# Merging a kernel's DMA transposes in pairs, with a new order of its work

## The chip, the cores and the metric

The kernel runs on one core of a Trainium2 chip. The metric is the device time of one execution in microseconds; three runs of the kernel before took 324.96, 324.96 and 325.57 us, the median is 324.96 us.

## The reference

One block of a transformer whose normalisations and residuals are modulated by a conditioning vector c. S = 2048 rows, D = 640, 32 heads of 20, F = 1536, all in bf16:

```python
mod = (silu(c) @ w_mod)            # six rows of 640: sa, ca, ga, sb, cb, gb
h = layernorm(x) * (1 + ca) + sa
q, k, v = split(h @ wqkv)          # 32 heads of 20
scores = q k^T / sqrt(20), masked to 0 <= i - j < 256
x = x + ga * (softmax(scores) v @ wo)
h = layernorm(x) * (1 + cb) + sb
x = x + gb * ((sigmoid(h @ w_gate) * (h @ w_up)) @ w_down)
```

## The kernel before, in words

**Tiling.** The 2048 rows are cut into 8 chunks of 256 rows, each of two blocks of 128. All weights lie in SBUF once they are loaded. Each chunk goes through these steps, and the steps of several chunks overlap:

- *ln1*: VectorE (DVE) takes each row's statistics (L773, L775), GpSimd (POOL) the power (L778, L780), and x is normalised (L793, or L790 on POOL).
- *hT*: the normalised rows are turned to 640 x 256. For chunks 0 to 2 (NPH = 3) TensorE (PE) does it; from chunk 3 on a DMA transpose for each block (transp_dma, L800, issued by SP). Then scale and shift are applied (modulate, L808 on ACT, L809 on DVE or POOL; L848/L849 where PE turned).
- *qkv*: chains of 5 matmuls (pe_chain, L686) project a block; ACT or DVE casts the result out of PSUM (evac, L884/L885): V into its tile, Q and K into stg, padded to 32 columns a head. stg is turned, for chunks 0 and 1 (NPQ = 2) by PE (matmuls on ident), else by one DMA transpose for Q into QT and one for K into KT.
- *attention*: sets of score matmuls into the one PSUM tile S (four banks); ACT takes the exponentials (E, L995), POOL masks the edges of the window (L1020), a burst of matmuls (pvs, M<-E,V) sums the values, DVE turns and divides (L1064, L1069, L1071, L1073). The rows are written to a DRAM buffer (doc) and read back turned (oT).
- *wo*, residual (L1125), *ln2*, and x2 turned into h2T by DMA transposes, two for each chunk.
- *mlp*: per pair of column tiles the chains g and u (M<-h2T,wg and M<-h2T,wu), tanh on ACT (L1170), the product hh on DVE ("glu", L1172), and at the chunk's end the down chains (M<-wd,hh), which need all of hh; then the residual (L1191) and the store.

**The modulation rows.** The first two (scale and shift of ln1) are needed at once: c is turned (L651), silu is formed (L653 to L655), spread over MW = 64 columns (silubc, L657), and fifty matmuls give mA ("modA"). The other four come in two groups in mod_rows: a group of 20 matmuls (modb, M<-wu,silubc and M<-hh,silubc), a transpose that gives shB or scB, and for the gate a scaled copy gq (L730), a DMA to a DRAM row (gate<-gq), and a DMA that reads this row onto all partitions (gbc<-gate). The first gate is multiplied into wo's five tiles (L1214), the second into wd's twelve (L1153), on DVE or POOL.

**What sets the order.** All operations and their engines stand in one table PRIO: the number of an operation gives its rank, its last digit (modulo 5) its engine. schedule() goes through them in that order, hands out the slots of the tile pools (M has four PSUM banks), and emit() writes each engine's program, with waits on semaphores. Each engine works off its program in order; an instruction that waits holds up all behind it. Nearly all DMAs are issued by SP, a few by ACT; a tile's slot passes on only when its last reader is done.

Of the kernel before, what the change touches and what calls it, by code (L numbers as in the profile page):

```python
# [8 lines left out]
ALU = mybir.AluOpType  # L9
# [352 lines left out]
def c_pe(n):  # L362
# [117 lines left out]
]  # L480
TR1 = 2
NPH = 3
NPQ = 2
PQ = ()
KEEP = 3
DSAFE = 0.3
RING = 256
FETCH = 3.3
START = 0.8
PORTLAG = 0.05  # L490
# [776 lines left out]
```

## Time and profile before

| what | value |
|---|---|
| median of 3 runs | 324.96 us |
| profiled execution, its own time | 324.87 us |
| its span in the trace | 323.1 us |
| granted TensorE clock | 1.00 |
| busiest engines | PE 317.6 us, ACT 216.1, DVE 210.0, POOL 177.3 |
| DMA issues on SP that transpose | 50 |

The span is the time from the first to the last recorded instruction; the execution's own time is 1.8 us longer. Times in the trace count from the span's start. PEld is PE's load of the stationary operand, which runs beside the matmuls; an engine with a "q" is its queue, where DMAs are issued. In a row of the timeline stand start, duration, engine, line, operation, tiles written and read, shape, count, and in brackets the idle time before it with what ended it.

### The profile page before, as it was taken

Reading aid. Unit: us, or ns where it says so; the run is one execution under the profiler, and the core shown is the slowest. Engines: PE = TensorE matmul, PEld = TensorE weight load, DVE = VectorE, ACT = ScalarE, POOL = GpSimd, SP = SyncE. Lnnn points to the kernel's source line nnn. Section 1 sums busy time; section 2 is a strip of 40 time slices with the busy share of each in tenths; the row PEclk is TensorE's granted clock in tenths of the full one; section 3 lists DMA queues with packets and bytes.
Section 4 is the critical chain, followed back from the end, with each engine's and each line's share of the span. In section 5 each row is a group of like instructions: output and inputs, shape, how many; then the busy total and the mean of one; then the engine's idle time right before and its main releaser. Section 6 shows DMA issues by size and latency. Waiting matters only on the chain.

```text
span 323.1 us, 11621 instructions
## 1 busy us (share of the span) xinstructions
PE 317.6 (98%) x4879; PEld 223.5 (69%) x4879; DVE 210.0 (65%) x420; ACT 216.1 (67%) x322; POOL 177.3 (55%) x267
## 2 busy tenths in 40 slices
PE   8999999999999999999999999999999999999997
PEld 3665545556776578766776567877786788877885
DVE  3799987897789856784757365647554576473332
ACT  2697887888766879976869877867778764112220
POOL 4146869868749593948393947582749273012000
PEclk9999999999999999999999999999999999999999
DMA  7989698989962275524325363410311021303001
GB/s 250 372 291 374 131 199 178 136 201 331 228 100 69 63 104 124 104 47 116 93 47 77 97 115 90 109 46 4 87 49 50 27 42 59 109 0 84 20 22 41
DMA packets 71039, 37.85 MB, mean 117 GB/s; under 512 B 45259, under 2 KB 69067, under 8 KB 70987
## 3 DMA queue, kind: packets, MB, share of 16 engines
q1 hardware_dynamic: 69680, 35.64, 46.1%
q10 hardware_dynamic: 1306, 1.48, 1.5%
q8 instruction: 38, 0.62, 0.8%
q14 instruction: 15, 0.11, 0.1%
HBM read 21.30 MB, written 5.25 MB: 82 GB/s over the span
## 4 chain that ended last, share of the span: by engine, by line
PE 90%; DVE 3%; DMA 2%; POOL 2%; issue 2%; ACT 1%; DVEq 0%; POOLq 0%
PE M L686 73%; PE S L687 7%; PE M L687 6%; PE S L666 2%; POOL E L1020 1%; DMA gbc<-gate 1%; DMA gate<-gq 1%; PE S L686 1%; ACT E L995 0%; POOL st L780 0%; DVE hh L1172 0%; DVE x L793 0%; DVE stg L885 0%; DVE KT L885 0%; DVE wo L1214 0%
## 5 line engine op out<-in xcount | busy, mean ns | idle before, releaser
L995 ACT ACTIVATE E<-S 128x512 bf16<-128x512 f32 (+2 forms) x184 | 150.2, 877 | 40.0 <-PE S L687 35.9
L1020 POOL TENSOR_SCALAR_AFFINE_SELECT E<-E 128x512 bf16<-128x512 bf16 (+1 forms) x176 | 138.8, 818 | 67.2 <-ACT E L995 30.1
L686 PE MATMUL M<-wqkv,hT 128*128 128x480 bf16 (+1 forms) x340 | 71.5, 355 | 0.9 <-DVE hT L809 0.6
L686 PE MATMUL M<-h2T,wg 128*128 128x256 bf16 x480 | 64.1, 273 | 0.0
L686 PE MATMUL M<-h2T,wu 128*128 128x256 bf16 x480 | 63.5, 273 | 0.0
L1172 DVE SCALAR_TENSOR_TENSOR hh<-sig,M 128x512 bf16<-128x512 f32 x48 | 32.0, 677 | 40.3 <-ACT sig L1170 29.6
L686 PE MATMUL M<-wd,hh 128*128 128x320 bf16 (+2 forms) x396 | 57.2, 295 | 0.2
L1170 ACT ACTIVATE sig<-M 128x512 f32<-128x512 f32 x48 | 28.7, 599 | 39.7 <-PE M L686 31.7
L686 PEld LDWEIGHTS M<-h2T,wg 128*128 128x128 bf16 x480 | 45.8, 98 | 7.4 <-issue 0.2
L686 PEld LDWEIGHTS M<-wqkv,hT 128*128 128x128 bf16 x340 | 30.8, 98 | 28.4 <-DMA wqkv<-in_A_wqkv_dram 0.9
L686 PEld LDWEIGHTS M<-h2T,wu 128*128 128x128 bf16 x480 | 45.4, 98 | 6.8 <-issue 0.2
L686 PEld LDWEIGHTS M<-wd,hh 128*128 128x128 bf16 x396 | 37.1, 98 | 14.5 <-DVE hh L1172 0.9
L1191 DVE TENSOR_TENSOR x<-M,x 128x320 bf16<-128x320 f32 (+2 forms) x33 | 15.3, 474 | 28.6 <-PE M L686 28.3
L687 PEld LDWEIGHTS S<-QT,KT 20*64 20x64 bf16 (+1 forms) x1856 | 19.9, 100 | 19.8 <-issue 8.4
L687 PE MATMUL S<-QT,KT 20*64 20x256 bf16 (+5 forms) x1856 | 32.1, 228 | 0.0
L773 DVE BATCH_NORM_STATS2 st<-x 128x6 f32<-128x320 bf16 x64 | 28.7, 479 | 3.5 <-DMA x<-in_A_x_dram 3.1
L1064 DVE STREAM_TRANSPOSE T<-M 128x512 f32<-128x512 f32 x32 | 21.1, 694 | 7.2 <-PE M L687 7.1
L686 PE MATMUL M<-wo,oT 128*128 128x320 bf16 x160 | 24.9, 299 | 0.0
L687 PE MATMUL M<-E,V 128*32 128x128 bf16 (+1 forms) x960 | 22.8, 246 | 0.5 <-DVE shB L738 0.3
L687 PEld LDWEIGHTS M<-E,V 128*32 128x32 bf16 x960 | 19.0, 97 | 4.9 <-POOL E L1020 2.4
L778 POOL TENSOR_SCALAR st<-st 128x2 f32<-128x2 f32 x16 | 3.6, 226 | 32.6 <-DVE st L775 31.8
L1125 DVE TENSOR_TENSOR x<-M,x 128x320 bf16<-128x320 f32 x32 | 15.5, 486 | 8.3 <-PE M L686 7.7
(75 smaller groups left out, 240.8 us busy)
## 6 DMA issues: line engine op xcount, KB each, us to landing
x<-in_A_x_dram SPq DMA_DIRECT2D x21, 160.0 KB, 3.5
doc<-On SPq DMA_DIRECT2D x64, 40.0 KB
wd<-in_B_w_down_dram SPq DMA_DIRECT2D x4, 480.0 KB, 4.3
out_dram<-x SPq DMA_DIRECT2D x11, 160.0 KB, 1.8
wd<-in_w_mod_dram SPq DMA_DIRECT2D x5, 320.0 KB
wqkv<-in_A_wqkv_dram SPq DMA_DIRECT2D x4, 400.0 KB, 7.9
wu<-in_w_mod_dram SPq DMA_DIRECT2D x5, 320.0 KB
oT<-doc SPq DMA_DIRECT2D x8, 192.0 KB, 2.5
```

What stands on the lines that cost most here:

```text
L666: ins = e.matmul(p_S.aps[0][:, 3, :], Eall[:, 0, 0:128], Eall[:, 0, 128:640], start=True, stop=True)
L686: return e.matmul(o, l, r, start=st, stop=sp, skip_group_check=True)
L687: return e.matmul(o, l, r, start=st, stop=sp, tile_position=tp, skip_group_check=True)
L773: A("dve", lambda e, g, bi=bi, j=j: e.bn_stats(v(bi * 12 + j * 6, 6), src[bi].ap[:, j * 320:(j + 1) * 320]), 0.48, reads=[src[bi].r()], wr ...
L778: A("pool", lambda e, g: e.tensor_scalar(v(28, n), var(), EPS, None, op0=ALU.add), 0.2, reads=[st.r(("m", bi)) for bi in range(n)], writes ...
L995: A("act", lambda e, eng: e.activation(dst(), src(), ACT.Exp, scale=SM_SCALE), c_act(n), reads=[Sp.r()], writes=[E.r(key)], prio=3, tag=f" ...
L1020: A("pool", lambda e, eng: e.affine_select(rows(dst), rows(src), pattern=[[0, 8], [sign, n]], compare_op=ALU.is_ge, fill=0.0, base=base, c ...
L1064: A("dve", lambda e, g, h=h: e.transpose(T1.ap[:, 512 * h:512 * h + 512], X[h].ap), 0.694, reads=[X[h].r()], writes=[T1.r(h)], prio=3.5, t ...
L1125: A("dve", lambda e, g, ps=ps, bi=bi, half=half: e.tensor_tensor(x1[bi].ap[:, half * 320:half * 320 + 320], ps.ap[:, 0:320], x1[bi].ap[:, ...
L1170: A("act", lambda e, g, pg=pg, sg=sg: e.activation(sg.ap[:], pg.ap[:], ACT.Tanh, scale=0.5), c_act(512), reads=[pg.r()], writes=[sg.r()], ...
L1172: A("dve", lambda e, g, pu=pu, sg=sg, f0=f0: e.scalar_tensor_tensor(out=hh.ap[:, f0:f0 + 2, :], in0=sg.ap[:].rearrange("p (a b) -> p a b", ...
L1191: A("dve", lambda e, g, ps=ps, bi=bi, c0=c0, n=n: e.tensor_tensor(x1[bi].ap[:, c0:c0 + n], ps.ap[:, 0:n], x1[bi].ap[:, c0:c0 + n], op=ALU. ...
```

## The change

- **hT and h2T**: one DMA transpose turns both blocks of a chunk, instead of one for each. The tiles are laid out [128, block, 5, 128] instead of [128, 5, 256], so operations on 256 columns now see two pieces of 128. x0 and x2 lie in one buffer each, whose slots are handed out in pairs (pairup).
- **Q and K**: one DMA transpose turns Q and K of a block, from two neighbouring stg slots into one tile QK that holds both. The pools QT (3) and KT (4) become one pool QK (4).
- **x** from chunk 3 on is read by one DMA per chunk.
- **Small buffers** are saved: MW is 32 instead of 64, cth lives in Dr, and gq in a slot of sig. A small load ("touch") into sig's second slot is issued by ACT; that slot is free only after it.
- **PRIO** is a new table. The count of operations on PE stays at 920 and of matmuls at 4880; ACT has 333 operations (331), DVE 422 (420), POOL 249 (255), SP 173 (200).

The core of the diff:

```diff
-    138, 143, 233, 128, 653, 33, 1593, 183, 573, 398, 38, 243, 318, 112, 163, 578, 151, 49, 166, 54, 59, 64, 69, 74,
+    83, 88, 193, 1173, 318, 983, 1008, 223, 1438, 313, 918, 287, 178, 278, 113, 598, 3466, 46, 4, 151, 24, 14, 19, 34,
...
-MW = 64
+MW = 32
...
-    p_hT = sbpool("hT", 2, [128, NDT, CH])
-    p_h2 = sbpool("h2T", 2, [128, NDT, CH])
+    p_hT = sbpool("hT", 2, [128, 2, NDT, 128])
+    p_h2 = sbpool("h2T", 2, [128, 2, NDT, 128])
...
-    p_QT = sbpool("QT", 3, [128, NG, CH])
-    p_KT = sbpool("KT", 4, [128, NG, CH])
+    p_QK = sbpool("QK", 4, [128, 2 * NG, CH])
...
+    def pairup(u, v):
+        u.mate, v.mate, v.odd = v, u, 1
...
+    touch = p_sig.aps[1][:].bitcast(BF16)
+    dma(lambda: touch[0:10, 0:32], lambda: w_mod[0:640:64, 0:32], 0.02, writes=[R("touch")], prio=-1, eng="act", nonc=True, tag="touch")
+    p_sig.init[1].append(P.ops[-1])
...
-        A("dve", lambda e, g: e.tensor_scalar(gq[:], ps.ap[:, 160 * gate:160 * gate + 160], factor, None, op0=ALU.mult), c_dve(160),
-          reads=[ps.r()], writes=[R_gq], prio=8, tag="gq")
+        gt = Tile(p_sig, "gq")
+        gq = lambda: gt.ap[:].bitcast(BF16)
+        A("dve", lambda e, g: e.tensor_scalar(gq()[:, 0:160], ps.ap[:, 160 * gate:160 * gate + 160], factor, None, op0=ALU.mult), c_dve(160),
+          reads=[ps.r()], writes=[gt.r()], prio=8, tag="gq")
...
-                ap = dst.ap[:, dt, :]
+                ap = dst.ap[:, :, dt, :]
...
-            turned[a] = [transp_dma(lambda bi=bi: t.ap[:, :, bi * 128:(bi + 1) * 128], lambda bi=bi: src[bi].ap[:], 4, 0.29,
-                                    [src[bi].r()], [t.r(("t", bi))], 1.26, f"atr{a}") for bi in range(2)]
+            turned[a] = [transp_dma(lambda: t.ap[:].rearrange("p b t c -> p (b t) c"),
+                                    lambda: x0all[:, src[0].slot:src[0].slot + 2, :].rearrange("p b c -> p (b c)"), 4, TW1,
+                                    [x.r() for x in src], [t.r(("t", bi)) for bi in range(2)], 1.28, f"atr{a}")]
...
-                else:
-                    transp_dma(lambda dst=dst, bi=bi: dst.ap[:, :, bi * 128:bi * 128 + 128], lambda s=s: s.ap[:], 3, 0.87,
-                               [s.r(i) for i in range(4)], [dst.r((bi, 0)), dst.r((bi, 1))], 1.28, f"qkt{a}")
+                elif g0:
+                    transp_dma(lambda dst=dst, bi=bi: dst.ap[:, :, bi * 128:bi * 128 + 128],
+                               lambda sq=sq: bass.AP(stgall, sq.slot * 1024, [[4096, 128], [1, 2048]]), 3, TW2,
+                               [x.r(i) for x in (sq, sk) for i in range(4)], [dst.r((g, bi, h)) for g in (0, NG) for h in range(2)], 1.6, f"qkt{a}")
...
-                    ps.ap[:, i * CH:(i + 1) * CH], w[:, kt, (f0 + i) * 128:(f0 + i + 1) * 128], h2.ap[:, kt, :]))
+                    ps.ap[:, i * CH:(i + 1) * CH], w[:, kt, (f0 + i) * 128:(f0 + i + 1) * 128], h2.ap[:, :, kt, :]))
```

What the new table moves, at the places where waits were found in the trace. First DVE's program where the first gate is multiplied into wo; M is the PSUM pool, T<-M x2 the two transposes of chunk 0's second pvs, stg and V the casts of chunk 2's projections. Before:

```order
L809 TENSOR_SCALAR hT<-hT,mA 128x256
L1064 STREAM_TRANSPOSE T<-M 128x512 x2
L1069 RECIPROCAL Dr<-T 128x32
L1071 TENSOR_TENSOR Tn<-T,Dr 128x32x20
L885 CAST stg<-M 128x24x20
L885 CAST V<-M 128x8x20
L1214 TENSOR_TENSOR wo<-wo,gbc 128x640 x2
L885 CAST stg<-M 128x24x20
L730 TENSOR_SCALAR gq<-M 128x160
```

And after, at the same place of DVE's program (sig in the first row is the second gate's gq):

```order
L734 TENSOR_SCALAR sig<-M 128x160
L741 STREAM_TRANSPOSE T<-M 128x160
L742 TENSOR_SCALAR scB<-T 128x5
L1078 STREAM_TRANSPOSE T<-M 128x512 x2
L1228 TENSOR_TENSOR wo<-wo,gbc 128x640
L897 CAST stg<-M 128x16x20
L897 CAST V<-M 128x8x20
L1083 RECIPROCAL Dr<-T 128x32
L1085 TENSOR_TENSOR Tn<-T,Dr 128x32x20
L1228 TENSOR_TENSOR wo<-wo,gbc 128x640 x2
```

The first scaling of wo now stands ahead of the casts stg and V, and of the reciprocal; the second gate's gq, which stood behind the first two scalings, stands ahead of the two transposes. SP's queue around the first gate, before:

```order
L800 DMA_TRANSPOSE hT<-x 128x5x128 x2
L588 DMA doc<-On 20x4x256 x3
L588 DMA wd<-in_B_w_down_dram 128x3x640
L588 DMA doc<-On 20x4x256
L587 DMA gate<-gq 4x5x32
L588 DMA gbc<-gate 128x640
L588 DMA x<-in_A_x_dram 128x640 x2
```

And after:

```order
L804 DMA_TRANSPOSE hT<-x 128x10x128
L586 DMA wu<-in_B_w_up_dram 128x2x768
L585 DMA gate<-sig 4x5x32
L586 DMA wg<-in_B_w_gate_dram 128x3x768
L586 DMA doc<-On 20x4x256
L586 DMA gbc<-gate 128x640
L586 DMA doc<-On 20x4x256 x2
```

A load of w_gate's half now stands between the gate's two transfers, and one of w_up ahead of them. Last, PE's program at the end of chunk 6's mlp, before (the last u chain of chunk 6, then down matmuls, of which the first eight are chunk 6's and need no product of that u chain):

```order
L686 MATMUL M<-h2T,wg 128x256 x6
L686 MATMUL M<-wd,hh 128x320 x16
L686 MATMUL M<-h2T,wg 128x256 x4
L686 MATMUL M<-h2T,wu 128x256 x10
L686 MATMUL M<-wd,hh 128x320 x40
L686 MATMUL M<-h2T,wg 128x256 x6
```

And after, where the first twelve of the 44 belong to chunk 5:

```order
L690 MATMUL M<-h2T,wg 128x256 x6
L690 MATMUL M<-wd,hh 128x320 x12
L690 MATMUL M<-h2T,wu 128x256 x6
L690 MATMUL M<-wd,hh 128x320 x44
L690 MATMUL M<-h2T,wg 128x256 x2
```

Between the last u matmul and the first down matmul that needs its product stood 8 matmuls, and 20 stand there now.

More of the change, by code (lines that the diff above doesn't have):

```diff
@@ L503 @@
 QMAX = 4.5
+TW1, TW2 = 1.0, 2.0
 PAIR = 0
@@ L530, in build @@
     c_col = sb("c_col", [128, NDT])
-    cth = sb("cth", [128, NDT], F32)
     siluc = sb("siluc", [128, NDT])
@@ L537, in build @@
     gbc = sb("gbc", [128, D])
-    gq = sb("gq", [128, 160])
-    mhalf = sb("mhalf", [128, 4], F32)
-    p_x0 = sbpool("x0", 4, [128, D])
-    p_x2 = sbpool("x2", 2, [128, D])
+    mhalf = sb("mhalf", [128, 2], F32)
+    x0all, x2all = sb("x0", [128, 4, D]), sb("x2", [128, 2, D])
+    p_x0 = Pool("x0", [x0all[:, i, :] for i in range(4)])
+    p_x2 = Pool("x2", [x2all[:, i, :] for i in range(2)])
     p_x1 = sbpool("x1", 6, [128, D])
-    p_hT = sbpool("hT", 2, [128, NDT, CH])
-    p_h2 = sbpool("h2T", 2, [128, NDT, CH])
+    p_hT = sbpool("hT", 2, [128, 2, NDT, 128])
+    p_h2 = sbpool("h2T", 2, [128, 2, NDT, 128])
     stgall = sb("stg", [128, 4, 1024])
     p_stg = Pool("stg", [stgall[:, i, :] for i in range(4)])
-    p_QT = sbpool("QT", 3, [128, NG, CH])
-    p_KT = sbpool("KT", 4, [128, NG, CH])
+    p_QK = sbpool("QK", 4, [128, 2 * NG, CH])
     p_V = sbpool("V", 8, [128, H * VW + 10])
@@ L561, in build @@
     p_Dr = sbpool("Dr", 1, [128, 32], F32)
+    cth = p_Dr.aps[0][:, 0:NDT]
     p_oT = sbpool("oT", 1, [128, NDT, CH])
@@ L566, in build @@
     p_sig = sbpool("sig", 2, [128, 512], F32)
-    p_st = sbpool("st", 3, [128, 34], F32)
+    stall = sb("st", [128, 3, 34], F32)
+    p_st = Pool("st", [stall[:, i, :] for i in range(3)])
     p_S = Pool("S", [nc.alloc_psum_tensor("S0", [128, 4, 512], F32)])
@@ L653, in build @@
     A("dve", lambda e, g: e.tensor_scalar(c_col[:], psc.ap[:, 0:NDT], 0.5, None, op0=ALU.mult), 0.17, reads=[psc.r()], writes=[R_ccol], prio=0)
-    A("act", lambda e, g: e.activation(cth[:], c_col[:], ACT.Tanh), 0.2, reads=[R_ccol], writes=[R_cth], prio=0)
-    A("dve", lambda e, g: e.scalar_tensor_tensor(out=siluc[:], in0=cth[:], scalar=1.0, in1=c_col[:], op0=ALU.add,
-                                                 op1=ALU.mult), 0.2, reads=[R_cth, R_ccol], writes=[R_siluc], prio=0)
+    A("act", lambda e, g: e.activation(cth, c_col[:], ACT.Tanh), 0.2, reads=[R_ccol], writes=[R_cth], prio=0)
+    p_Dr.init[0].append(A("dve", lambda e, g: e.scalar_tensor_tensor(
+        out=siluc[:], in0=cth, scalar=1.0, in1=c_col[:], op0=ALU.add, op1=ALU.mult), 0.2, reads=[R_cth, R_ccol], writes=[R_siluc], prio=0))
     A("act", lambda e, g: e.activation(silubc[:], siluc[:].unsqueeze(2).to_broadcast([128, NDT, MW]), ACT.Copy), c_act(NDT * MW),
@@ L729, in mod_rows @@
               tag="modb", mode=2, ni=8 * NDT)
-        A("dve", lambda e, g: e.tensor_scalar(gq[:], ps.ap[:, 160 * gate:160 * gate + 160], factor, None, op0=ALU.mult), c_dve(160),
-          reads=[ps.r()], writes=[R_gq], prio=8, tag="gq")
-        dma(lambda: row.rearrange("(t j c) -> j t c", j=4, c=32), lambda: gq[0:128:32, :].rearrange("j (t c) -> j t c", c=32), 0.1,
-            reads=[R_gq], writes=[R_row], prio=8, tag="gate", nonc=True)
+        gt = Tile(p_sig, "gq")
+        gq = lambda: gt.ap[:].bitcast(BF16)
+        A("dve", lambda e, g: e.tensor_scalar(gq()[:, 0:160], ps.ap[:, 160 * gate:160 * gate + 160], factor, None, op0=ALU.mult), c_dve(160),
+          reads=[ps.r()], writes=[gt.r()], prio=8, tag="gq")
+        dma(lambda: row.rearrange("(t j c) -> j t c", j=4, c=32), lambda: gq()[0:128:32, 0:160].rearrange("j (t c) -> j t c", c=32), 0.1,
+            reads=[gt.r()], writes=[R_row], prio=8, tag="gate", nonc=True)
         dma(lambda: gbc[:], lambda: row.unsqueeze(0).to_broadcast([128, D]), 0.42, reads=[R_row], writes=[R_gbc],
@@ L756, in fnA @@
             return pad(e, FILL) if kt < NDT - 1 else ins
-        oA.append(A("pe", fnA, MW / 2400.0 * 10 + (0.2154 * FILL if kt < NDT - 1 else 0.0), reads=[Rm[0][kt], R_silubc], writes=[psA.r()], prio=0, lat=0.2, tag="modA", ni=20 + 2 * FILL, extra=wprev))
+        oA.append(A("pe", fnA, 64 / 2400.0 * 10 + (0.2154 * FILL if kt < NDT - 1 else 0.0), reads=[Rm[0][kt], R_silubc], writes=[psA.r()], prio=0, lat=0.2, tag="modA", ni=20 + 2 * FILL, extra=wprev))
     p_E.init[0].extend(oA)
@@ L800, in fn @@
             return e.dma_start_transpose(dst(), src())
-        return A("sp", fn, dur, reads=reads, writes=writes, prio=prio, work=work, tag=tag, lat=0.08 + DSAFE, dlat=3.64 if work > 0.5 else 3.40)
+        return A("sp", fn, dur, reads=reads, writes=writes, prio=prio, work=work, tag=tag, lat=0.08 + DSAFE, dlat=3.64 if work > 1.5 else 3.40)
     def modulate(dst, sc, sh, Rmod, prio, ln, a, turned_by=None):
@@ L837, in cp @@
                 def cp(e, g, dt=dt, pv=pv):
-                    return e.activation(dst.ap[:, dt, :], pv(), ACT.Copy) if g == "act" else e.tensor_copy(dst.ap[:, dt, :], pv())
+                    o, i = dst.ap[:, :, dt, :], pv().rearrange("p (b c) -> p b c", b=2)
+                    return e.activation(o, i, ACT.Copy) if g == "act" else e.tensor_copy(o, i)
                 A(("act", "dve"), cp, {"act": c_act(256), "dve": c_dve(256)}, reads=[rp], writes=[dst.r(("t", dt))], prio=1, tag=f"{ln}turn{a}")
@@ L847, in ev @@
                 if g == "act":
-                    return e.activation(dst.ap[:, dt, lo:hi], pv()[:, lo:hi], ACT.Identity, scale=sc[:, dt:dt + 1], bias=sh[:, dt:dt + 1])
-                return e.tensor_scalar(dst.ap[:, dt, lo:hi], pv()[:, lo:hi], sc[:, dt:dt + 1], sh[:, dt:dt + 1], op0=ALU.mult, op1=ALU.add)
+                    return e.activation(dst.ap[:, :, dt, :], pv().rearrange("p (b c) -> p b c", b=2), ACT.Identity, scale=sc[:, dt:dt + 1], bias=sh[:, dt:dt + 1])
+                return e.tensor_scalar(dst.ap[:, :, dt, :], pv().rearrange("p (b c) -> p b c", b=2), sc[:, dt:dt + 1], sh[:, dt:dt + 1], op0=ALU.mult, op1=ALU.add)
             prev[dt] = [A(("act", "dve"), ev, {"act": 0.56, "dve": 0.53}, reads=[rp] + Rmod,
@@ L867, in ln1 @@
             for b in blocks:
-                x0[b] = load_x(p_x0, b, 0.55 if a < 4 else 20 + 0.1 * a, eng=XE, extra=turned[a - 2])
+                x0[b] = Tile(p_x0, f"x0_{b}")
+            pairup(x0[2 * a], x0[2 * a + 1])
+            ts = [x0[b] for b in blocks]
+            dma(lambda: x0all[:, ts[0].slot:ts[0].slot + 2, :], lambda: x_flat[a * CH:(a + 1) * CH, :].rearrange("(b p) c -> p b c", p=128),
+                0.94 if a < 4 else 1.2, writes=[t.r() for t in ts], prio=0.55 if a < 4 else 20 + 0.1 * a, tag=f"x{2 * a}", eng=XE,
+                lat=0.2 + DSAFE, extra=turned[a - 2])
             raw = [x0[b] for b in blocks]
@@ L909, in qkv @@
             pairs = [(lambda kt=kt, bi=bi, ps=ps, lo=lo, hi=hi: (
-                ps.ap[:, 0:hi - lo], hT[a].ap[:, kt, bi * 128:(bi + 1) * 128], wqkv[:, kt, lo:hi])) for kt in range(NDT)]
-            hold = ([sq, QT[a]] if lo < D else []) + ([sk, KT[a]] if hi > D and lo < 2 * D else []) + ([V[b]] if hi > 2 * D else [])
+                ps.ap[:, 0:hi - lo], hT[a].ap[:, bi, kt, :], wqkv[:, kt, lo:hi])) for kt in range(NDT)]
+            hold = ([sq, QK[a]] if lo < D else []) + ([sk, QK[a]] if hi > D and lo < 2 * D else []) + ([V[b]] if hi > 2 * D else [])
             name = "q" if lo < D else "k" if lo < 2 * D else "v"
@@ L924, in qkv @@
                      [V[b].r(i) for i in range(v // 160 - 8, hi // 160 - 8)], 6.5, f"evv{a}", extra=first)
-            for key, s, dst, end in (("q", sq, QT[a], D), ("k", sk, KT[a], 2 * D)):
+            for g0, s, end in ((0, sq, D), (NG, sk, 2 * D)):
+                dst = QK[a]
                 if not lo < end <= hi:
                     continue
-                if a < NPQ or (a, key, bi) in PQ:
+                if a < NPQ:
                     for half in range(2):
@@ L1131, in outproj @@
         x2 = [Tile(p_x2, f"x2_{2 * a + bi}") for bi in range(2)]
+        pairup(*x2)
         ln_stats(x1, x2, 7, "b", a)
@@ L1136, in outproj @@
         else:
-            for bi in range(2):
-                transp_dma(lambda bi=bi: h2.ap[:, :, bi * 128:(bi + 1) * 128], lambda bi=bi: x2[bi].ap[:], 2, 0.29,
-                           [x2[bi].r()], [h2.r(("t", bi))], 1.26, f"btr{a}")
+            transp_dma(lambda: h2.ap[:].rearrange("p b t c -> p (b t) c"), lambda: x2all[:].rearrange("p b c -> p (b c)"), 2, TW1,
+                       [x.r() for x in x2], [h2.r(("t", bi)) for bi in range(2)], 1.28, f"btr{a}")
             modulate(h2, scB, shB, [R_shB, R_scB], 7, "b", a)
```

19 lines of the change are left out of this document (9 added, 10 removed), and 220 rows, old and new, of the table PRIO.

## The prediction

> **What bounds the kernel now.** I read the page's busy shares first, then its chain that ended last, then the busy time by stage, then the chain piece by piece. The page says that TensorE (PE) is the bound, and that nearly all of the chain is PE's own work:
>
> ```profile
> PE 317.6 (98%) x4879; PEld 223.5 (69%) x4879; DVE 210.0 (65%) x420; ACT 216.1 (67%) x322; POOL 177.3 (55%) x267
> PE 90%; DVE 3%; DMA 2%; POOL 2%; issue 2%; ACT 1%; DVEq 0%; POOLq 0%
> ```
>
> The stages (start and end, us, PE busy with its instructions, granted clock, DMA share, GB/s) show where PE still waits:
>
> ```profile
> 0.00:11.10 11.10, 9.18 (x83) 1.00 0.85 281
> 11.10:34.00 22.90, 22.89 (x253) 1.00 1.04 327
> 34.00:46.00 12.00, 11.24 (x231) 1.00 0.75 162
> 46.00:70.00 24.00, 23.58 (x357) 1.00 0.94 186
> 70.00:271.00 201.00, 200.89 (x3542) 1.00 0.42 93
> 271.00:323.10 52.10, 49.79 (x442) 1.00 0.15 43
> ```
>
> From 70 to 271 us PE is idle for 0.11 of 201 us. Its instructions stay the same in kind and number, so whatever the merged transposes do there, they can gain next to nothing. What can move is the start (11.10), the gate stage 34 to 46 (0.76 idle), 46 to 70 (0.42 idle) and a few waits late; the last stage's 2.31 also holds the store after PE has ended. All the waits after 11.1 us together are worth some 2.5 us, so the forecast is a sum of small terms.
>
> **The merged transposes: 0.** The trace lists one issue's time on SP's queue (ns, least/median/most) and, for the last chunk, what follows the landing:
>
> ```profile
> L800 SPq DMA_TRANSPOSE h2T<-x x16: 1202/1212/1380, 67.0 to 291.4; - x16
> L800 SPq DMA_TRANSPOSE KT<-stg x12: 1231/1308/2696, 42.3 to 191.7; - x12
> 294.05 1.09 ACT L808 ACTIVATE h2T<-h2T,shB,scB 128x256 bf16<-128x256 bf16 x2 [1.69 <-DMA h2T<-x]
> 298.38 0.82 PE L686 MATMUL M<-h2T,wg 128*128 128x256 bf16 x6
> ```
>
> 25 of 50 issues go: 25 x 1.2 = 30 us of SP, which is not on the chain. In the tightest place, the last chunk, ACT waits 1.69 us for h2T, but PE reads it only at 298.38: over 3 us after the two modulations end at 295.14. A merged pair waits for its second half, but this second half is today issued only behind the first one's 1.2 us. So the landing moves by about a microsecond either way, inside that slack: 0, bounds -0.3 to +0.3 (if one landing late by a few hundred ns reaches PE). [...]
>
> **The moving operand in two pieces: 0.** mlp's h2T is now read as 2 x 128 columns 128 x 5 elements apart. The trace has a matmul whose moving operand is in ten pieces of 32 (modb, on wu), beside one of the same 320 columns in one piece:
>
> ```profile
> L687 PE MATMUL M<-wu,silubc 128*32 128x320 bf16 x20 | 0.9, 300 | 0.1
> L686 PE MATMUL M<-wo,oT 128*128 128x320 bf16 x160 | 24.9, 299 | 0.0
> ```
>
> 300 against 299 ns for ten pieces: I take 0 for two. The upper bound is 1 ns on each of 960 mlp matmuls, +1.0 us.
>
> **The gate stage: +1.4.** This is the term that decides. The chain there, piece by piece, and the instructions around it:
>
> ```profile
> 36.49 3.24 DMA gate<-gq
> 39.74 3.40 DMA gbc<-gate
> 43.24 0.50 DVE wo L1214
> 43.76 0.49 DVE wo L1214
> 44.25 0.58 DVE stg L885
> 44.88 2.50 PE M L686 x14
> ```
>
> ```profile
> 34.51 0.86 PE L687 MATMUL M<-wu,silubc 128*32 128x320 bf16 x20
> 35.75 0.28 DVE L730 TENSOR_SCALAR gq<-M 128x160 bf16<-128x160 f32 x1
> 39.05 1.31 DVE L1064 STREAM_TRANSPOSE T<-M 128x512 f32<-128x512 f32 x2
> 41.53 0.65 DVE L885 CAST stg<-M 128x480 bf16<-128x480 f32 x1
> 42.10 0.31 DVE L885 CAST V<-M 128x160 bf16<-128x160 f32 x1
> 43.05 1.18 PE L686 MATMUL M<-wqkv,hT 128*128 128x480 bf16 x5
> 44.88 0.28 PE L686 MATMUL M<-ident,stg 128*128 128x128 bf16 x2 [0.30 <-DVE stg L885]
> ```
>
> Before, DVE clears the two casts of chunk 2's projection (41.53, 42.10) ahead of the first wo scaling, which waits for gbc until 43.24. After, the first scaling stands ahead of both casts, so that projection's PSUM slot stays taken until gbc has landed. How late: counting each instruction of the new orders from 11.11 on at the pace of its like in the trace, modb starts about 0.35 us later in PE's new order and gq ends about 0.4 after the 36.03 of now. Then 0.46 to the gate's issue, 3.24, 3.40: gbc at about 43.6. Then wo 0.50, a stg cast of 320 columns some 0.5, V 0.31: the slot is free at 45.0. Before, PE started its next projection into such a slot at 43.05: 1.95 later. In the new order one more turning of four 128-column matmuls stands ahead of it, 0.2 that PE needs anyway; and the wait swallows what the kernel before loses after this point, the 0.30 at 44.88 and a little more, 0.35. 1.95 - 0.2 - 0.35 = **+1.4**. Bounds: 0, if gq and the gate's two transfers come that much sooner and the slot is free as PE arrives; +2.5, if the 576 KB of wg that now go out between the gate and gbc push gbc back by another microsecond. A second wait is new: the second gq shares one sig buffer with the first until a small "touch" load late in ACT's queue has run, so it waits for the gate's landing (40.1), and behind it on DVE stand the modulation rows' transpose and pvs0's two transposes (39.05 now, about 41 then). They are done before 43.6, so what they delay is hidden under the wait for gbc; if gbc came earlier, this wait would be next, and it alone would keep about +0.5. POOL's masks wait for the last of the three scalings, now behind recip and divide, about 47.2 against 44.4; two masks more are done ahead, so POOL is about 1 us behind, no more than PE.
>
> **46 to 70: -0.2.** PE's idle time here is 0.42 in all (the stage's row); chunk 4's projections and the second block's pvs fall into it, which wait for hT's modulation and for POOL's masks. With hT in one transpose and PE later by 1.4 I take off half; bounds -0.4 and +0.3 (masks later than PE).
>
> **Last glu to down: -0.55.** Down of a chunk needs the last glu, which needs the last mlp matmul:
>
> ```profile
> 291.76 0.61 ACT sig L1170
> 292.37 0.91 issue
> 293.28 0.70 DVE hh L1172
> 294.02 26.90 PE M L686 x232
> 292.65 2.63 PE L686 MATMUL M<-wd,hh 128*128 128x320 bf16 x16
> 314.20 2.88 PE L686 MATMUL M<-wd,hh 128*128 128x320 bf16 x20
> L686 PEld LDWEIGHTS M<-wd,hh 128*128 128x128 bf16 x396 | 37.1, 98 | 14.5 <-DVE hh L1172 0.9
> ```
>
> Twenty downs without a gap take 2.88 us (314.20), the last of them 0.30 for itself (the 299 ns above): 0.136 apart. In chunk 6 the down that needs the glu stands 8 matmuls behind the first (292.65 + 1.09 = 293.74) and starts at 294.02: 0.28 lost. At the same distance chunk 7 loses nothing (the twenty), so 8 is the edge. The last row's 0.9 is the sum of two such waits of the weight load, in chunks 3 and 6. The new order puts 20 downs of chunks 5 and 6 between in chunk 6, and 8 mlp matmuls and a score set in chunk 3: at least 1.5 us further off. -0.55, bounds -0.6 and 0 (should a wait come up in another chunk).
>
> **Start: -0.2.**
>
> ```profile
> 6.41 0.17 DVE L655 SCALAR_TENSOR_TENSOR siluc<-cth,c_col 128x5 bf16<-128x5 f32 x1 [0.28 <-ACT cth L654]
> 7.22 0.45 PE L686 MATMUL S<-silubc,wd 128*128 128x64 bf16 x10
> 7.51 0.38 PE L676 MATMUL S<-E 128*128 128x512 bf16 x1
> 11.11 0.43 PE L686 MATMUL M<-wqkv,hT 128*128 128x320 bf16 x2 [0.62 <-DVE hT L809]
> ```
>
> c is turned six warm-up matmuls into the program instead of ten, siluc no longer waits for it but for x's statistics (about 6.2), and silubc is half as wide. From 7.22 to 7.51 ten matmuls of 64 columns take 29 ns each; at half the time the 50 would save 0.7, at the same time nothing. Against that all five casts of hT now stand on ACT (four before). I take -0.2, bounds -0.7 and +0.35. [...]
>
> **Sum.** -0.2 + 1.4 - 0.2 - 0.55 = +0.45. The profiled execution took 324.87, the median of the runs is 324.96: **325.3 us**. What a measurement can tell from no change is about 0.2%, 0.65 us.
>
> **Rivals.** *Faster*: gbc is there as PE arrives, the gate stage costs what it costs now (0); the other terms remain: 324.87 - 0.95 = 323.9, and if half of the 0.76 goes too, 323.5. For it: the gate's transfer and gbc's took 3.24 and 3.40 under load, which can vary; against it: nothing in the change shortens either, and the second gq's wait alone holds half a microsecond. *Slower*: a large load now stands between the gate and gbc in SP's queue, with another ahead of the gate:
>
> ```profile
> wg<-in_B_w_gate_dram SPq DMA_DIRECT2D x2, 576.0 KB
> gate<-gq SPq DMA_DIRECT2D x2, 1.2 KB
> ```
>
> At the stages' 162 to 327 GB/s the 576 KB alone take 1.8 to 3.6 us, and gbc queues behind what is left of them. Place: 37 to 44 us; it decides once wg is still moving at 40.2, when gbc is issued. Price 1 to 2.4 us: 326.3 to 327.7. *The operand in pieces* does cost 1 ns or more on 960 matmuls: 326.3. *Nothing reaches PE*: SP's saving and all else is hidden, and the new waits are as long as the old: 324.9.
>
> **Chances.** Forecast (324.7 to 326.4) 0.42; faster rival 0.30; late gbc 0.14; operand 0.07; no effect 0.07. The forecast's spread lies half above 325.6, which is 0.2% over the median. Faster by over 0.2%: 0.30, the faster rival; within: 0.28, half the forecast and the case of no effect; slower: 0.42, the rest. The range leaves out the faster rival's far end and half of the slow one: 323.4 to 327.2.
>
> **What would show it.** Right: one wait of PE of 1.5 to 2.3 us near 43 to 45 us, ended by a DVE cast, with wo's first scaling (idle before it: gbc) just ahead; no wait of PE on hh in chunks 3 and 6; first projection at 10.9; PE's mlp pace unchanged. Wrong: gbc landing before 42.5, or after 44.5; the first scaling not waiting; mlp matmuls slower than 273 ns; new waits of PE on h2T or QK between 70 and 271 us.

## The result, and the profile after

The changed kernel took **328.62 us** (median of 4 executions, 327.47 to 329.95) against 324.96 (324.71 to 325.57) for the kernel before on the same chip: ratio 1.0110, interval 1.0083 to 1.0136. In a second session it took 327.86 (327.48 to 330.07), ratio 1.0099 (1.0068 to 1.0130). It is slower by 2.8 to 3.7 us; the forecast was 325.3, at most 327.2. The profiled execution took 327.47 us, its span is 325.7 us.

The page's busy shares and its chain that ended last, after. PE's share of the chain falls from 90% to 83%, DMA's rises from 2% to 6%:

```profile
PE 316.5 (97%) x4878; PEld 223.4 (69%) x4879; DVE 207.5 (64%) x422; ACT 218.1 (67%) x326; POOL 173.1 (53%) x261
PE 83%; DMA 6%; POOL 4%; DVE 3%; ACT 2%; issue 2%; SPq 0%; POOLq 0%; DVEq 0%
```

The same stages as in the prediction (start and end, length, PE busy, granted clock, DMA share, GB/s):

```profile
0.00:11.10 11.10, 8.19 (x82) 1.00 0.85 275
11.10:34.00 22.90, 21.20 (x228) 1.00 0.93 331
34.00:46.00 12.00, 10.89 (x221) 1.00 0.69 185
46.00:70.00 24.00, 22.98 (x343) 1.00 0.79 169
70.00:271.00 201.00, 200.92 (x3516) 1.00 0.43 92
271.00:325.70 54.70, 52.31 (x501) 1.00 0.18 46
```

PE's idle time grew by 1.69 us from 11.1 to 34 (0.01 before, 1.70 now) and by 0.95 from 34 to 70 (1.18 before, 1.11 + 1.02 now). Behind 70 us it stands still (0.11 and 2.31 before, 0.08 and 2.39 now). Ahead of 11.1 it grew by 0.99, but PE's work there shrank by as much, and the first projection starts where it did (11.14 us; 11.11 before). These 2.64 us are the whole difference of the two spans, 325.7 - 323.1 = 2.6. The waits of PE, longest first, name two new places:

```profile
PE M L690 <- DVE V L897: 1.7, 1, 1.7
PE M L691 <- DVE stg L897: 1.5, 1, 1.5
```

**The wait at 28 us** is the one that the prediction does not have. The timeline of PE, of DVE, and of ACT's queue:

```profile
28.07 0.84 PE L691 MATMUL M<-E,V 128*32 128x256 bf16 x32 [1.47 <-DVE stg L897]
```

```profile
22.30 0.88 DVE L777 BATCH_NORM_STATS2 st<-x 128x6 f32<-128x320 bf16 x2
26.26 0.89 DVE L777 BATCH_NORM_STATS2 st<-x 128x6 f32<-128x320 bf16 x2 [3.08 <-DMA x<-in_A_x_dram]
...
27.31 0.61 DVE L897 CAST stg<-M 128x480 bf16<-128x480 f32 x1
...
30.51 1.26 DVE L1078 STREAM_TRANSPOSE T<-M 128x512 f32<-128x512 f32 x2
```

```profile
19.09 0.44 ACTq L586 DMA_DIRECT2D x<-in_A_x_dram  x1
```

DVE stands idle for 3.08 us with the statistics of chunk 3 at its head, until the merged load of chunk 3's x has landed. Behind them in its order stand the cast of a projection that PE needs (27.31) and the transposes of pvs0 (30.51). The load was issued at 19.09 by **ACT**; in the kernel before, SP issued chunk 3's two loads. It took 7.15 us. The chain of waits carries it, as it does the gate behind it:

```profile
19.09 7.15 DMA x<-in_A_x_dram
...
38.49 2.70 DMA gate<-sig
41.20 4.34 DMA gbc<-gate
45.64 0.49 DVE wo L1228
46.13 0.41 DVE stg L897
46.57 0.33 DVE V L897
```

Why so long? SP's queue, before and then after. Before, nothing is issued from 13.6 to 17.60: SP stands at chunk 3's x itself, which the kernel lets go only behind a step of chunk 1's turning on PE. After, that wait is ACT's, and SP runs on without a stop and sends the weights ahead of the x load:

```profile
13.15 0.43 SPq L588 DMA_DIRECT2D hh<-in_w_mod_dram  x1
17.60 0.33 SPq L588 DMA_DIRECT2D x<-in_A_x_dram  x1
```

```profile
12.73 1.38 SPq L586 DMA_DIRECT2D wu<-in_w_mod_dram  x3
14.15 0.44 SPq L586 DMA_DIRECT2D wo<-in_A_wo_dram  x1
14.63 2.28 SPq L586 DMA_DIRECT2D wu<-in_w_mod_dram  x2
```

From 9 to 26 us the queues of the kernel after moved (packets, MB, share of 16 engines; q1 is SP's, q10 ACT's):

```profile
q1 hardware_dynamic: 5272, 6.05, 101.6%
q10 hardware_dynamic: 272, 0.33, 5.5%
```

The DMA engines are full (101.6 + 5.5%), and ACT's single load of 320 KB stands beside 6 MB of SP's. None of its packets moves before 22.75 us, 3.7 us after the issue. Then they move beside SP's, nearly as many of the one as of the other, and the load takes until 26 us (the queues from 23 to 25 us):

```profile
q1 hardware_dynamic: 230, 0.49, 66.8%
q10 hardware_dynamic: 215, 0.27, 39.0%
```

**The wait at 47 us** is the predicted one. PE, after:

```profile
46.95 2.20 PE L690 MATMUL M<-wqkv,hT 128*128 128x480 bf16 x10 [1.69 <-DVE V L897]
```

The chain above shows its cause as forecast: the first scaling of wo waits for gbc until 45.64, and the casts stg and V behind it hold the projection's slot.

### The profile page after: what moved, and what is told of

Its sections match the earlier page's. It is cut to its first block, busy times and chain, and to the rows that moved or that the text cites. A ratio compares the mean times of both kernels' runs of the same rounds, so it can differ in the third digit from the quotient of the medians.

```text
span 325.7 us, 11547 instructions
## 1 busy us (share of the span) xinstructions
PE 316.5 (97%) x4878; PEld 223.4 (69%) x4879; DVE 207.5 (64%) x422; ACT 218.1 (67%) x326; POOL 173.1 (53%) x261
## 4 chain that ended last, share of the span: by engine, by line
PE 83%; DMA 6%; POOL 4%; DVE 3%; ACT 2%; issue 2%; SPq 0%; POOLq 0%; DVEq 0%
PE M L690 69%; PE S L691 7%; PE M L691 6%; POOL E L1034 3%; DMA x<-in_A_x_dram 2%; DMA wd<-in_w_mod_dram 2%; DMA gbc<-gate 1%; ACT E L1009 1%; DMA gate<-sig 1%; DVE st L777 1%; POOL x L794 1%; DVE stg L897 1%; PE S L690 0%; DVE wo L1228 0%; DVE hh L1186 0%
## 5 line engine op out<-in xcount | busy, mean ns | idle before, releaser
L690 PE MATMUL M<-h2T,wg 128*128 128x256 bf16 x480 | 66.7, 273 | 0.0
L690 PE MATMUL M<-h2T,wu 128*128 128x256 bf16 x480 | 65.3, 273 | 0.0
L690 PE MATMUL M<-wd,hh 128*128 128x320 bf16 (+2 forms) x396 | 56.5, 295 | 0.0
L691 PEld LDWEIGHTS S<-QK 20*64 20x64 bf16 (+1 forms) x1856 | 19.9, 100 | 19.5 <-ACT E L1009 8.7
L691 PE MATMUL S<-QK 20*64 20x256 bf16 (+5 forms) x1856 | 32.1, 228 | 0.1
L1087 DVE STREAM_TRANSPOSE On<-Tn 128x1024 bf16<-128x1024 bf16 x16 | 19.8, 1236 | 0.2
```

Of the source, the lines that this page charges most:

```text
L690: return e.matmul(o, l, r, start=st, stop=sp, skip_group_check=True)
L691: return e.matmul(o, l, r, start=st, stop=sp, tile_position=tp, skip_group_check=True)
L1087: A("dve", lambda e, g: e.transpose(On.ap[:], Tn.ap[:]), 1.22, reads=[Tn.r()], writes=[On.r()], prio=4, tag=f"tr2_{a}")
```

## The experiments

The theory from the comparison: *x queue*, the late load of chunk 3's x, costs about 2 us; *gate order*, the first scaling ahead of the casts, about 1.3 us; the rest of the change nothing. Rivals: DVE's order as such (where the statistics stand), the start, the load of wg ahead of gbc, the merged transposes themselves. In the edits PRIO[n] is the rank and engine of operation n, and `place` puts operations behind another one without changing their engines. Intervals are of the ratio to the kernel before, run in the same session.

**e1_stats_late**: chunk 3's statistics and power behind chunk 0's divide on DVE, and the normalisation behind a later cast.

```diff
+place(PRIO, [284, 283, 285, 281, 280, 282, 286, 287, 288], 316)
+place(PRIO, [290], 172)
```

> The changed kernel with chunk 3's layer-norm statistics (and the power and normalisation behind them) placed later in DVE's and POOL's order: behind the casts and transposes that PE waits for at 28 to 31 us. Theory L (load): the merged x load of chunk 3 lands 7 us after its issue, DVE's statistics wait for it and hold up a stg cast and pvs0's transposes, which cost PE 1.5 + 0.3 us; then the waits at 28.07 and 31.23 are gone, modb and the gate come that much earlier, and the time falls by 1.5 to 2 us, to 325.5 to 326 for the short executions (327.5 now). Theory G (gate): only the order at wo's scaling and the later gate matter, the earlier waits are swallowed there; then the wait at 47 us grows by what is won before, and the time stays within 0.5 us of 327.5.

328.99 us, ratio 1.0118 (1.0077 to 1.0160). The wait at 28 us is gone, but PE now waits 1.13 us at 36.9 and 1.47 at 41.5, for work that stands behind the moved statistics on DVE. A miss for the simple form of the theory: the load stays late, and the time that DVE loses to it shows at another place.

**e2_wos_late**: the three scalings of wo that come first, behind chunk 0's second transposes.

```diff
+place(PRIO, [217, 218, 219], 343)
```

> The changed kernel with the first three scalings of wo placed on DVE behind recip, divide, chunk 2's casts and the transpose of pvs0's result. Theory G: PE's wait of 1.85 us at 47 us is gone and the time falls by 1.3 to 1.9 us, to about 325.8 (short executions). Theory L: the kernel still pays 1.8 us at 28 to 31 us, so it stays about 1 us above the kernel before. If neither scaling nor load matters and the longer time comes from all over (slower matmuls on the operand in two pieces), the time stays at 327.5 and more.

327.48 us, 1.0069 (1.0046 to 1.0093). The wait at 47 us is gone, the one at 28 us stays (1.41), and PE waits 0.68 us anew at 56 us for POOL, which stands behind the later scalings. So moving all three gives part of the gain back.

**e3_both**: e1 and e2 in one kernel.

```diff
+place(PRIO, [284, 283, 285, 281, 280, 282, 286, 287, 288], 316)
+place(PRIO, [290], 172)
+place(PRIO, [217, 218, 219], 343)
```

> Both edits at once. If the two waits add up as the trace says (1.54 + 0.35 at 28 to 31 us, 1.85 at 47 us, against some 1.0 that the kernel before loses at its own gate stage), the time is about 324.2, level with or just under the kernel before (324.96). If one wait only hides the other, it stays near the better of the two single edits, about 325.8.

329.71 us, 1.0125 (1.0087 to 1.0162): no gain, since both new waits come together (1.14 at 37.0, 0.90 at 42.5, 0.69 at 58). Curing a wait by moving its victims only moved it.

**e4_x_on_sp**: the x load of chunk 3 goes from ACT to SP at the same rank; nothing else.

```diff
+PRIO[279] += 3
```

> The changed kernel with chunk 3's merged x load issued by SP (at its old rank, ahead of three of w_mod's loads) instead of ACT; DVE's order is untouched. Theory L, queue part: on ACT's queue the load shares the DMA engines with some 3 MB that SP has already issued; on SP it stands ahead of most of them and lands about 22.5 instead of 26.2, the wait at 28 us is gone, 1.5 to 2 us less, as in the experiment that moves the statistics. If it is the merge itself (320 KB in one load) that makes it late, it still lands after 24.5 and the gain is under 0.7 us.

326.40 us (7 executions), 1.0040 (1.0017 to 1.0063). SP issues the load at 19.51, and the statistics follow without a wait:

```profile
19.51 0.38 SPq L587 DMA_DIRECT2D x<-in_A_x_dram  x1
```

```profile
22.73 1.66 DVE L778 BATCH_NORM_STATS2 st<-x 128x6 f32<-128x320 bf16 x4
```

At most 3.22 us from issue to landing, instead of 7.15. But the load does not meet the same backlog here: it waits on SP for the same step of PE and holds SP's queue from 14.04 to 19.51, much as in the kernel before. By then the transfers have run nearly dry (19 to 20 and 20 to 21 us; the kernel after moved 392 and 380 GB/s there):

```profile
19.00:20.00 1.00, 1.00 (x17) 1.00 0.49 186
20.00:21.00 1.00, 1.00 (x12) 1.00 0.41 70
```

The wait at 28 us is gone; the gate's stays:

```profile
45.12 2.20 PE L691 MATMUL M<-wqkv,hT 128*128 128x480 bf16 x10 [1.44 <-DVE V L898]
```

So 2.2 us of the 3.7 by the medians (1.5 of the 2.8 of the second session) hang on which engine issues one load, and so on whether SP is held there.

**e6_wo_behind**: e4, and the first scaling of wo behind stg, V, reciprocal and divide.

```diff
+PRIO[279] += 3
+place(PRIO, [217], 342)
```

> The changed kernel with the x load on SP (as in the earlier experiment, 326.4) and the first scaling of wo placed on DVE behind the two casts of chunk 2, recip and divide, with its two fellows. Theory G: PE's wait of 1.6 us at 45 us falls to 0.3 or less, as in the kernel before, and the time to about 325.1. Rival: POOL, which may not pass the scalings, or the second gq's wait for the gate takes over, and at least 1 us of wait comes back between 45 and 60 us; then 326.

325.33 us (10 executions), 0.9998 (0.9981 to 1.0015). Both waits are gone in the stages too (11.1 to 34, and 34 to 46):

```profile
11.10:34.00 22.90, 22.90 (x257) 1.00 0.94 331
34.00:46.00 12.00, 11.70 (x228) 1.00 0.85 208
```

Another 1.1 us. With two operations moved, the changed kernel takes what the kernel before takes: a third cause, if there is one, is within the interval, some half a microsecond.

**e7_wg_late**: e4, and the second half of w_gate behind gbc on SP.

```diff
+PRIO[279] += 3
+place(PRIO, [65], 210)
```

> The changed kernel with the x load on SP (326.4) and the 576 KB load of wg moved from between the gate and gbc to behind gbc in SP's queue. Theory Q (queue): that load makes gbc's transfer 4.2 us long instead of 3.4; with it behind, gbc takes 3.4, lands at 42.9, and the wait at 45 us is shorter by 0.8: 325.6. Rival: gbc's length comes from something else (the w_up load ahead of the gate, the doc writes), it stays above 4 us and the time stays at 326.4.

326.99 us (6 executions), 1.0067 (1.0036 to 1.0098), not below e4. gbc's transfer fell from 4.17 us in e4 to 3.85, PE's wait for the gate from 1.44 to 1.02, and small waits came up elsewhere (0.34 at 51 us, for QK). The load between gate and gbc, the prediction's slower rival, makes gbc some 0.3 us longer; it is not what makes the kernel slower.

**e5_wmod_order**: the first three slices of w_mod loaded in the order in which PE reads them.

```diff
+PRIO[20], PRIO[21], PRIO[22] = 14, 19, 24
```

> The changed kernel with one edit: SP loads w_mod's first five slices in the order in which PE reads them (the changed kernel issues slices 1 and 2 ahead of 0, and PE begins with 0, which lands at 7.5 to 8.1 us). Theory S (start): that slice is the last thing the first projection hangs on; with it first, the first modA group starts when silubc is there, about 7.0, and the first projection at 10.7 to 10.9 instead of 11.1 to 11.75; the time falls by 0.3 to 0.8 us. Rival: the fifth slice (9.1 to 9.5) and the casts of hT set the start anyway; then the projection stays at 11.1 or later and the time does not move by more than the scatter.

328.01 us, 1.0091 (1.0064 to 1.0118); the first projection starts at 11.37. No gain, though PE's wait for w_mod ahead of the first slice's matmuls (1.01 us in the kernel after) is gone: the chain to the first projection now runs over chunk 0's x load (1.37 to 5.40 us), its statistics and its normalisation.

**e8_before_h2t**: the kernel before with h2T alone turned by one transpose per chunk, in the new layout.

```diff
+for s in (2023, 1822, 1621, 1390, 1140, 890, 640, 374):
+    PRIO[s:s + 2] = [max(PRIO[s:s + 2])]
...
-    p_h2 = sbpool("h2T", 2, [128, NDT, CH])
+    p_h2 = sbpool("h2T", 2, [128, 2, NDT, 128])
...
+            transp_dma(lambda: h2.ap[:].rearrange("p b t c -> p (b t) c"), lambda: x2all[:].rearrange("p b c -> p (b c)"), 2, 1.0,
...
```

> The kernel before, in its own order, with only the h2T transposes merged (one for both blocks, at the later one's place, h2T in the new layout, so that mlp's moving operand is in two pieces). The prediction's view: nothing on PE's path moves, 325.0 within 0.5 us, SP's issues take 8 x 1.35 instead of 16 x 1.21 us, mlp matmuls stay at 273 ns. Rival (operand in pieces): mlp's matmuls come 1 ns or more further apart, 1 to 3 us more in all. Rival (merge delays): some h2T comes later than PE needs it, a wait of PE on h2T shows.

324.83 us (10 executions), 0.9983 (0.9965 to 1.0000). Merging costs nothing, nor does the operand in two pieces: the mlp matmuls stay at 273 ns.

```profile
L689 PE MATMUL M<-h2T,wg 128*128 128x256 bf16 x480 | 64.1, 273 | 0.0
```

**e9_x_act_sp_held**: the changed kernel, x on ACT as it is, but SP is held ahead of the third slice of w_mod's next part (12.75 to 19.6 us) until the step of chunk 1's turning on PE for which the x load waits too.

```diff
+    P.ops[33].deps.append(P.ops[159])
     P.schedule()
```

> The changed kernel, chunk 3's x load still on ACT's queue, but SP held before its third slice of w_mod's second group until chunk 1's last turning by PE, the same point for which the x load waits; so SP has little outstanding when the x load is issued. Theory C (contention): the load was late because some 3 MB stood in SP's queue; now it lands 3 to 4 us after its issue (22.5 to 23.5), the wait at 28 us is gone, and the time is that of the x load on SP, 326.4. Rival: ACT's queue itself is slow for it; it still takes 6 to 7 us and the time stays near 328.

326.49 us (10 executions), 1.0049 (1.0017 to 1.0081). ACT issues the load at 19.30, and DVE's idle time ahead of the statistics shrinks from 3.08 to 0.23:

```profile
19.30 0.43 ACTq L586 DMA_DIRECT2D x<-in_A_x_dram  x1
```

```profile
23.62 0.89 DVE L777 BATCH_NORM_STATS2 st<-x 128x6 f32<-128x320 bf16 x2 [0.23 <-DMA x<-in_A_x_dram]
```

4.3 us on ACT's queue when SP has sent less ahead (207 and 154 GB/s from 19 to 21 us): what made the load slow was what SP had queued, 2.85 us of the 7.15, not ACT. Its packets move from 21.25 us on, 2.0 us after the issue, and 249 of 272 from 22 to 23. PE's wait at 28 us is gone. The median is pulled up by three executions of 329.6 to 330.0 us with a granted clock of 0.994 or 0.995; the other seven took 324.8 to 326.9. The profiled one, 329.95, is one of the three: PE waits 3.15 us for V behind the gate there, and the clock is 0.50 from 48 to 50 us. In the kernel after, 215 packets of ACT's queue moved beside 230 of SP's from 23 to 25 us, but the first moved only 3.7 us after the issue, 2.0 in e9. A queue of its own did not spare the load the backlog: 7.15 us with it and 4.3 with less of it.

**e10_before_x_on_act**: the reverse, in the kernel before: chunk 3's two unmerged x loads go to ACT.

```diff
+PRIO[280] -= 3
+PRIO[281] -= 3
```

> The kernel before with one edit: chunk 3's two x loads issued by ACT instead of SP (two loads, not merged, all else as it was). Theory L/C: SP no longer waits there and runs ahead with its loads, the two x loads land at about 26 instead of 20.2 and 23.3, chunk 3's statistics hold up DVE, and the time rises by 1 to 2 us to 326 to 327. If it was the merge that made the load late, the time stays at 325.2 within 0.5.

329.53 us, 1.0145 (1.0118 to 1.0172). Neither the merge nor the new order is needed for the loss. The loads no longer hold SP's queue, they land late, and PE waits 3.9 us:

```profile
22.87 6.27 DMA x<-in_A_x_dram
```

```profile
PE M L689 <- POOL st L782: 3.9, 1, 3.9
```

The loss is larger than the wait alone explains; the clock behind it is taken up below.

**e11_best**: e8 with the last downs moved behind other work and the scalings of wo behind a cast.

```diff
+place(PRIO, [1221], 1758)
+place(PRIO, [1903], 1715)
+place(PRIO, [216, 217], 252)
```

> The kernel before with h2T merged (324.83) and three moves in its order: in chunks 3 and 6 the down step that needs the last glu stands 0.36 us (a score set) and 1.6 us (twelve downs) later, and the first two scalings of wo stand behind the next stg cast. The prediction's price of these waits (0.27, 0.28 and 0.37 us in the trace): the time falls by 0.9 us to 324.0. Rival: what is won there is lost at the next wait (pvs1 for POOL's masks at 69 us, behind the scalings); then 324.5 to 324.8.

324.78 us (12 executions), 0.9993 (0.9978 to 1.0007). The waits for the last glu go, and no difference can be measured. No version tried clearly beats the kernel before.

**a_again**: the changed kernel once more, unedited.

> The changed kernel once more, unedited, for its scatter and a second profile: 327.4 to 330, as in its first four executions. If its place-to-place differences come from transfers, this profile's losses sit at 28, 47 us and at waits for DMAs later on, not in slower instructions.

327.48, 327.77 and 327.94 us, and the profiled one 330.07. In that execution gbc took 5.46 us instead of 4.34, PE waited 2.8 us instead of 1.7 for V, and then (46 to 48, 48 to 52 us, granted clock in the fifth column):

```profile
PE M L690 <- DVE V L897: 2.8, 1, 2.8
```

```profile
46.00:48.00 2.00, 0.00 (x0) 0.86 0.43 158
48.00:52.00 4.00, 3.96 (x35) 0.64 0.83 158
```

The granted clock is 0.64 for 4 us behind the wait. The same in e10, behind its 3.9 us (28 to 32, 32 to 36 us): 0.50 over 4 us.

```profile
28.00:32.00 4.00, 0.12 (x9) 0.85 0.62 238
32.00:36.00 4.00, 4.00 (x45) 0.50 0.21 41
```

Does the wait pull the clock down? The last four runs put one wait of chosen length into a quiet stretch of the kernel before, at 200 us: DVE takes n more statistics whose results nobody uses, and a g chain waits for the last of them.

```diff
+    scr = sb("scr", [128, n, 6], F32)
+    stats, mlp = P.ops[1380], P.ops[1161]
+    first = stats.fn
+    def longer(e, g):
+        first(e, g)
+        for i in range(n):
+            last = e.bn_stats(scr[:, i, :], wo[:, 0, 0:320])
+        return last
+    stats.fn = longer
+    stats.deps.extend(o for o in P.ops if o.tag == "wos")
+    mlp.deps.append(stats)
```

**d6_wait** (n = 6):

> The kernel before, with one wait of PE put into the quiet middle of the program: six more statistics of 0.45 us each on DVE behind one at 198.5 us, and a g chain that starts at 200.4 us waits for the last of them. PE should wait some 1.35 us (199.0 + 6 x 0.45 = 201.7, less 200.4). Both theories (a wait costs its own length; a wait beyond a length of about 3 us is followed by a spell of lower granted clock) expect the same: 1.2 to 1.5 us more than before, the granted clock at 1.00 throughout.

**d8_wait** (n = 8):

> The same with eight more statistics: a wait of about 2.25 us. If the clock falls only behind waits of 3 us and more, as the executions with waits of 1.85, 2.99 and 3.94 us suggest, then 2.1 to 2.4 us more than before at a clock of 1.00. If the lower clock belonged to shorter waits too, about 1.5 us beyond that.

**d10_wait** (n = 10):

> The same with ten more statistics: a wait of about 3.15 us. If a wait of 3 us and more pulls the granted clock down for some microseconds: 4.5 to 5.2 us more than before (the wait and 1.4 to 2 us of slower matmuls), and slices behind 200 us with a clock under 0.9. If the slow spells of the other runs had nothing to do with the wait: 3.1 us more, clock 1.00.

**d13_wait** (n = 13):

> The same with thirteen more statistics: a wait of about 4.5 us. With the clock pulled down behind it: 6 to 6.5 us more than before, if the price of the spell is the same at any length of the wait, more if it grows with it. Without: 4.5 us more, clock 1.00.

| run | wait of PE, us | ratio to before | executions at clock 1.00, us | executions at 0.99 to 0.995, us |
|---|---|---|---|---|
| d6_wait | 1.00 | 1.0008 (0.9989 to 1.0026) | 10: 324.9 to 326.3 | none |
| d8_wait | 1.78 | 1.0038 (1.0019 to 1.0057) | 7: 326.0 to 326.8 | 3: 327.3 to 327.7 |
| d10_wait | 2.57 | 1.0098 (1.0064 to 1.0131) | 2: 327.6 | 2: 328.9, 329.1 |
| d13_wait | 3.75 | 1.0146 (1.0115 to 1.0176) | none | 4: 329.0 to 330.5 |

The wait is that of the profiled execution, and 0.35 to 0.75 us shorter than I had worked out. Only this one execution of each kernel has a trace; that PE waited as long in the others is not shown. The stretches of d8's profile (200 to 202, 202 to 204, 204 to 206 us; the clock behind the count) and d13's (204 to 206, 206 to 208):

```profile
200.00:202.00 2.00, 0.27 (x24) 1.00 0.22 56
202.00:204.00 2.00, 1.95 (x26) 0.55 0.41 129
204.00:206.00 2.00, 2.00 (x69) 0.59 0.03 8
```

```profile
204.00:206.00 2.00, 1.42 (x22) 0.80 0.00 0
206.00:208.00 2.00, 2.00 (x56) 0.50 0.03 8
```

The wait does pull the clock down, to 0.55, 0.56 and 0.50 in the lowest 2 us of d8, d10 and d13, and for some 4 us. My edge of 3 us was wrong: it is no edge, but a chance that grows with the wait: 0 of 10 at 1.0 us, 3 of 10 at 1.8, 2 of 4 at 2.6, 4 of 4 at 3.75. Nor is 1.8 us an edge. In the profiled execution of e3 the clock fell behind a wait of 1.14 us, with waits of 0.28 and 0.20 in the 3 us ahead of it (38 to 40 us below; 0.77 in the two us before, 0.87 in the two behind); in e1's, with the same waits up to 37 us, it stayed at 1.00.

```profile
38.00:40.00 2.00, 2.00 (x38) 0.50 0.59 109
```

The price can be read within one kernel: in d8 the median of the executions at 0.995, 327.57, less that of the others, 326.14, is 1.4 us, if they waited equally long; in d10 328.98 - 327.59 is 1.4.

## Why the prediction was wrong, point by point

- **The step that failed: x was given no term.** The prediction's list of what can move ("the start (11.10), the gate stage 34 to 46 (0.76 idle), 46 to 70 (0.42 idle) and a few waits late") leaves the stage from 11.10 to 34 out, and its sum has no term for the x load; the runs showed 1.69 us more idle time of PE there. That x is read by one DMA per chunk stood in the change, but the prediction nowhere says which engine issues it, and a load that leaves SP's order was not counted. SP is also no longer held at 13.6 to 17.60 us, and as its queue ran ahead the transfers from 18 to 20 us rose from 219 GB/s before to 389 after (DMA share 0.72 and 1.04). e4 (-2.2 us), e9 and e10 (the same loss in the kernel before) show it. That this stage has no idle time in the kernel before (0.01 us) was read as nothing to gain; it also meant that nothing there hid a late input: PE waited 1.47 us for the cast behind it.
- **The gate stage: right in mechanism and nearly in size.** Forecast +1.4 with one wait of 1.5 to 2.3 us, ended by a DVE cast behind the first scaling. Measured 1.69 against 0.30, and e6 gains 1.1 us. Its time was not as forecast: gbc landed at 45.54 (41.20 + 4.34) instead of 43.6, after the 44.5 that the prediction had named as a sign of being wrong, as everything came later behind the first wait and gbc's transfer took 4.34 instead of 3.40. In e4, without the first wait, gbc lands at 43.72 (39.55 + 4.17), as forecast, but by luck: the gate took 2.73 instead of 3.24 and gbc 4.17 instead of 3.40, and the two errors nearly cancel.
- **46 to 70: right in sign only at a second look.** PE's idle time there is 1.02, of which 0.95 is the tail of the gate's wait (46.00 to 46.95). The remaining 0.07, against 0.42 before, is a gain of 0.35; forecast was 0.2.
- **The last glu: right in the trace, too small for the clock.** DVE's hh ends no wait of the weight load any more, and the last 49 us of the chain up to the final residual are one unbroken piece of PE:

```profile
274.70 48.63 PE M L690 x416
```

  But e11, which removes the same two waits from the kernel before, is not measurably faster.
- **The start: 0 instead of -0.2.** The first projection stands at 11.14, against 11.11; in other runs with the new order it stood between 11.09 and 11.75. Ten matmuls of 32 columns take 0.25 us (7.99 to 8.24), ten of 64 took 0.29 (7.22 to 7.51), so the fifty save 0.2 us, not 0.7. e5 shows that the order of the first slices does not set the start.
- **The merged transposes: 0 is right, the saving on SP is not what I counted.** e6 has all of them and is level with the kernel before. Times of one issue after (ns, least, median, most):

```profile
L804 SPq DMA_TRANSPOSE QK<-stg x12: 1702/2476/3613, 46.6 to 192.3; - x12
L804 SPq DMA_TRANSPOSE h2T<-x x8: 1278/1352/2332, 70.6 to 294.4; - x8
L804 SPq DMA_TRANSPOSE hT<-x x5: 1263/1443/2782, 34.9 to 130.3; - x5
```

  A merged Q and K takes 2.48 us, the two separate ones took 1.31 + 1.25: nothing saved. h2T and hT do save, 8 x (2 x 1.21 - 1.35) + 5 x (2 x 1.25 - 1.44) = 13.9 us, not 30. No wait of PE between 70 and 271 us came of it.
- **The operand in two pieces: 0, right.** 273 ns (e8).
- **The clock was missing.** Waits were priced at their own length. Of the eight executions of the changed kernel two, 329.95 and 330.07, had a granted clock of 0.995, and the median of the other six is 327.74: in the one with a trace the gate's wait grew to 2.8 us, and the slower clock came on top. One execution, 329.52, is long at a clock of 1.00; it has no trace, and why stays open.

The sum for the profiled executions, in PE's idle time: 0 (start) + 1.69 (x) + 0.95 (34 to 70) = 2.6, the difference of the two spans; the forecast for the same stages was 0 (x) + 1.2.

What stays open: why no packet of the load on ACT's queue moves for 3.7 us beside SP's full queue. How the load would fare on SP's own queue behind such a backlog was not run: in e4 SP had been held.

## What to carry to other kernels

When a schedule changes, list each load with its issuing engine and what the other queue sends in the microseconds ahead of it: here SP, freed of a wait, sent its transfers sooner, and beside them the one load that PE's next work hung on took 7.15 us. Where a stage shows no idle time at all, look for what could come late there, not only for what could be gained. And price a wait of the TensorE beyond its own length: here 1.4 us more once the clock has fallen, which it did in a share of the executions that grew with the wait, in one even behind 1.14 us.

## What the runs showed of the hardware that was not expected

- A 320 KB load took 7.15 us on ACT's queue beside a full SP queue, 4.3 us with SP held (e9), and at most 3.22 us on SP's queue when that had run nearly dry (e4, up to the statistics that read it). Beside the full queue its first packet moved 3.7 us after the issue; from 23 to 25 us 215 of its packets moved beside 230 of SP's.
- The granted clock fell to 0.50 to 0.64 for some 4 us behind waits of PE of 1.14 to 3.9 us, in a share of executions that grew with the wait, and cost 1.4 us (d8, d10).
- One DMA transpose of Q with K takes 2.48 us to issue, as much as the two it replaces (1.31 + 1.25); the merged x2 takes 1.35 us against 1.21 for one half.
